# Float32 products of one transform stage replaced by three products of 12-bit parts

## The chip, the cores and the metric

One core of one Trainium2 chip. The metric is the device time of one execution in microseconds (us), lower is better. Runs of one kernel are compared by their medians.

## The reference

Two independent layers on inputs of 2048 positions and 512 features; their outputs are concatenated.

```python
def _A_ref(x, dft_seq_re, dft_seq_im, dft_hid_re, dft_hid_im):
    a = jnp.einsum("bsd,ed->bse", x, dft_hid_re)
    b = jnp.einsum("bsd,ed->bse", x, dft_hid_im)
    return jnp.einsum("ts,bse->bte", dft_seq_re, a) - jnp.einsum("ts,bse->bte", dft_seq_im, b)

def _B_ref(u, log_A_real, A_imag, C_real, C_imag, log_dt, D_skip):
    L = u.shape[1]
    dt = jnp.exp(log_dt)
    A = -jnp.exp(log_A_real) + 1j * A_imag
    C = (C_real + 1j * C_imag) * dt[:, None]
    P = jnp.exp((A * dt[:, None])[:, :, None] * pos[None, None, :])
    K = 2.0 * jnp.einsum("dn,dnl->dl", C, P).real
    Kf = jnp.fft.rfft(K, 2 * L)
    Uf = jnp.fft.rfft(u_t, 2 * L)
    y = jnp.fft.irfft(Uf * Kf[None, :, :], 2 * L)[:, :, :L]
    return y.transpose(0, 2, 1) + u * D_skip[None, None, :]
```

A multiplies x by two given matrices from both sides. B builds a long convolution kernel K from 128 exponentials per feature and convolves u with it. u has 2048 x 512 float32 values.

## The kernel before

Both layers run at once on the core. The Python program simulates a schedule while it emits instructions: each piece of work is a generator that yields either an event or a semaphore to wait for, or a pair of an engine and an assumed duration. `Plan.run` takes, again and again, the piece that can start first, and among those of equal start the one of lower urgency number (line 125). The order of the instructions on every engine is thus fixed by these assumed durations when the program is written; at run time each engine's queue runs in that order and waits on hardware semaphores. A generator's urgency is the second argument of `spawn`.

**Layer A, class `Fnet`.** Eight groups of sequence products ("s", sixteen blocks of 128 each) and four groups of hidden products ("p", eight blocks each). Every float32 operand is split into a high part rounded to the type `float32r` (ACT, line 184) and the rest, also `float32r` (DVE, line 188). Three products, high by high, high by low and low by high, are added in PSUM (line 304): one block of the moving operand is used for four 128-column slices of the stationary one, so twelve matmuls of 128x128 by 128x512. x is split once and stays in SBUF; the matrices stream through. `loads` (line 242) holds a buffer named "uk" of B's pool for x in flight, four blocks deep, and gives it back (`b.uks`, line 239) when all sixteen blocks of x are split. Splits have urgency 0, or 3 when three blocks or more are split ahead; the matmuls have urgency 5, and fill PE whenever nothing else is ready.

**Layer B, class `Ssm`.** In order of dependence:

- `tables` (urgency 2) with `seed_args` (1), `seeds`, `tables1` and `tables2`: for each of sixteen chunks of 32 features, powers of the exponentials, built on DVE by products and sums (lines 543 and 552) from seeds on ACT (lines 586 to 604) and their signed copies (line 618).
- `taps`: the values of K, sixteen times 128 small matmuls (line 739); `stage1_k`: the first transform stage of K (line 769) and its store.
- `spectrum_u` (urgency 2) and `stage1_u` (urgency 1), the part that is changed: the first transform stage of u. There are eight groups k. A group loads an eighth of u (512 KB, line 808) into one of two halves of a tile, takes two PSUM buffers of two banks each, does four float32 matmuls (line 814), evacuates them on ACT (four activations of 128x512, line 824), and stores them (line 830). The matrix `f1u` is stacked twice over the partitions, and the two halves of the rows work on different data: `tile_position=(64 * r, 0)`, each into its own bank.
- `products`: for four quarters h of the features and four parts q: loads (line 867), the second stage on PE (line 894), the complex product on DVE (lines 909 to 922), the first inverse stage (line 929) and a store (line 950).
- `inverses`: load, last stage (line 975), evacuation and store of the output (line 984).

B has two PSUM buffers in all, shared by `taps`, `stage1_k`, `stage1_u`, `products` and `inverses`; `banks` (line 415) hands them out in the order of asking. Of the buffers "uk", "z", "zl" and "xt" in B's pool there is one each until the tables are done, and two each in a second pool after that. `products` needs "uk" too.

All loads and most stores go through SP's queue, in the order of the plan.

Of the kernel before, what the change touches and what calls it, by code (L numbers as in the profile page):

```python
# [8 lines left out]
F32 = mybir.dt.float32  # L9
F32R = mybir.dt.float32r  # L10
I32 = mybir.dt.int32
AF = mybir.ActivationFunctionType
OP = mybir.AluOpType
# [3 lines left out]
SEQ, DM, NS = 2048, 512, 128  # L17
# [128 lines left out]
def act(cols):  # L146
    return 0.09 + cols * 0.00085


def dve(cols, rate=1.0):  # L150
    return (62 + cols / rate) / 960


def load(kb):
    return max(0.55, kb / 330)
# [210 lines left out]
class Ssm:  # L366
# [38 lines left out]
    def constants(self, which, ev):  # L405
        yield "dma", sum(load(4 * math.prod(a.shape) / 1024) for _, _, a in self.cst[which])
        for n, t, a in self.cst[which]:
            self.nc.sync.dma_start(t, a)
            setattr(self, n, t)
        if ev is self.const_ev:  # L410
            yield "dve", 0.3
            self.nc.vector.tensor_scalar(self.dskip, self.dskip, 0.5, None, op0=OP.mult)
        self.plan.set(ev)
# [376 lines left out]
    def spectrum_u(self):  # L790

        self.uleft = 16
        yield self.const_ev
        b = self.sets[0]
        yield b.zls
        self.xu_sb, self.xus = b.pool.tile([128, 2, 2, DM], F32, name="zl", bufs=b.n), Sem(2)
        for k in range(8):
            name = "uk"[k % 2]
            yield b.xts[name]
            if not k:  # L800
                self.u_sb = b.pool.tile([128, 2, 2, DM], F32, name="xt", bufs=b.n)
            self.plan.spawn(self.stage1_u(k, name), 1)

    def stage1_u(self, k, name):
        nc, b = self.nc, self.sets[0]
        u = self.u_sb[:, k % 2]
        yield "dma", load(512)
        nc.sync.dma_start(u, self.uG[:, 2 * k:2 * k + 2])
        got = yield from self.banks(2)
        yield "pe", 1.82  # L810
        for m in range(2):
            for r in range(2):
                rows = slice(64 * r, 64 * r + 64)
                nc.tensor.matmul(got[m][1][:, r], self.f1u[rows], u[rows, m], start=True, stop=True,  # L814
                                 tile_position=(64 * r, 0))
        self.plan.put(b.xts[name])
        for m in range(2):
            n = 2 * k + m
            sem = b.zbs if n % 3 == 2 else self.xus
            yield sem  # L820
            x = b.pool.tile([128, 2, DM], F32, name="z", bufs=b.n) if n % 3 == 2 else self.xu_sb[:, n % 3]
            for r in range(2):
                yield "act", act(512)
                nc.scalar.activation(x[:, r], got[m][1][:, r], AF.Copy)
            self.give(got[m][0])
            self.plan.spawn(self.store_u(x, 2 * k + m, sem), 1)

    def store_u(self, x, m, sem):
        yield "dma", load(512)
        self.nc.sync.dma_start(self.xu.rearrange("s c l d -> (s c) l d")[:, 2 * m:2 * m + 2], x)  # L830
        self.plan.put(sem)
        self.uleft -= 1
        if not self.uleft:
            self.plan.put(self.sets[0].zls)
            self.plan.set(self.xu_ev)

    def quarters(self):
# [225 lines left out]
```

## Time and profile before

| | us |
|---|---|
| median of 3 runs | 588.68 |
| lowest, highest | 588.62, 590.52 |
| the profiled execution | 590.22 |
| its span in the profile | 588.4 |

The profile shows one execution. PE is TensorE, PEld its weight loads, DVE VectorE, ACT ScalarE, POOL GpSimd, SP the engine whose queue issues the transfers. `L814` is line 814 of the kernel. A row of a group names the line, engine, operation, output and inputs by the program's names (tiles of one pool that share a name show as one: u in SBUF is `xt`, and the PSUM buffers are `f`), the shape, the count, the busy time and the mean of one in ns, and then the idle time of the engine just ahead of them with what ended it. A float32 matmul shows as two records. In the order of time a row has start, duration, engine, line, operation, and in brackets the idle time ahead of it. In the chain of waits a row has start, duration and what ran.

The granted clock of PE is 1.00 throughout.

### The profile page before, as it was taken

How to read it: one execution, taken by the hardware profiler on the slowest of the kernel's cores; microseconds unless marked ns; L12 is line 12 of the kernel's file. 1: busy time of each engine (PE TensorE's matmuls, PEld its weight loads, DVE VectorE, ACT ScalarE, POOL GpSimd, SP SyncE). 2: the span in 40 equal slices, each digit the busy share in tenths (PEclk: the TensorE clock that was granted, in tenths of full speed). 3: DMA queues.
4: the chain of work that ended last, by engine and by line, in shares of the span. 5: the costliest groups of instructions: out<-in, count | busy, mean ns of one | idle time of the engine just before them, and what ended most of it. 6: DMA issues, size and time to landing. Idle time of an engine off the chain costs nothing.

```text
span 588.4 us, 14902 instructions
## 1 busy us (share of the span) xinstructions
PE 580.2 (99%) x5958; PEld 439.7 (75%) x5958; DVE 496.5 (84%) x883; ACT 380.8 (65%) x745; POOL 4.7 (1%) x12
## 2 busy tenths in 40 slices
PE   8999999999999999999999999999999999999997
PEld 6767668778778777877687778777877776876785
DVE  7986989999999999999999999999999954245420
ACT  4789884946676677758674876577764635264622
POOL 0000000000000000000000000000000000000000
PEclk9999999999999999999999999999999999999999
DMA  8999996363493369446768684559798744998674
GB/s 262 329 367 338 337 342 199 101 188 81 122 280 106 89 170 264 137 135 165 246 183 259 168 246 128 136 158 284 225 282 234 230 131 148 283 354 263 190 251 144
DMA packets 141238, 125.84 MB, mean 214 GB/s; under 512 B 46192, under 2 KB 106352, under 8 KB 140912
## 3 DMA queue, kind: packets, MB, share of 16 engines
q1 hardware_dynamic: 140880, 124.48, 69.4%
q8 instruction: 47, 0.77, 0.5%
q10 hardware_dynamic: 288, 0.39, 0.2%
q14 instruction: 23, 0.19, 0.1%
HBM read 82.12 MB, written 42.73 MB: 212 GB/s over the span
## 4 chain that ended last, share of the span: by engine, by line
PE 69%; DVE 21%; issue 4%; DMA 3%; ACT 2%; SPq 1%; DVEq 0%; ACTq 0%
PE acc L304 52%; DVE prod L543 7%; DVE lo L188 4%; DVE t L552 4%; PE f L894 4%; PE f L739 3%; PE f L814 3%; PE f L975 3%; PE f L929 2%; PE f L769 2%; DMA xt<-xk 1%; DVE t L572 1%; DMA raw<-in_sT 1%; DVE t L566 1%; DVE cs L613 1%
## 5 line engine op out<-in xcount | busy, mean ns | idle before, releaser
L304 PE MATMUL acc<-hi,x_hi 128*128 128x512 f32 x640 | 257.2, 402 | 0.5 <-ACT x_hi L184 0.4
L304 PE MATMUL acc<-lo,x_hi 128*128 128x512 f32 x640 | 250.1, 391 | 1.5 <-issue 1.3
L304 PE MATMUL acc<-hi,x_lo 128*128 128x512 f32 x640 | 249.5, 390 | 0.1
L543 DVE TENSOR_TENSOR prod<-t,cs 128x1024 f32<-128x1024 f32 (+4 forms) x192 | 163.3, 869 | 3.6 <-ACT t L681 1.5
L188 DVE TENSOR_TENSOR lo<-raw,hi 128x512 fp32r<-128x512 f32 x160 | 109.1, 686 | 56.8 <-ACT hi L184 54.6
L304 PEld LDWEIGHTS acc<-hi,x_hi 128*128 128x128 f32 x640 | 120.1, 188 | 49.2 <-issue 21.2
L184 ACT ACTIVATE hi<-raw 128x512 fp32r<-128x512 f32 x160 | 100.1, 628 | 85.8 <-PE acc L304 64.7
L304 PEld LDWEIGHTS acc<-hi,x_lo 128*128 128x128 f32 x640 | 120.2, 188 | 28.0 <-issue 1.5
L304 PEld LDWEIGHTS acc<-lo,x_hi 128*128 128x128 f32 x640 | 120.2, 188 | 23.8 <-DVE lo L188 0.9
L552 DVE TENSOR_TENSOR t<-prod 128x512 f32<-128x512 f32 (+4 forms) x192 | 94.3, 510 | 1.1
L559 ACT ACTIVATE square<-t 128x256 f32<-128x256 f32 (+1 forms) x64 | 36.6, 572 | 24.6 <-DVE t L552 22.5
L327 ACT ACTIVATE y<-acc 128x512 f32<-128x512 f32 x47 | 27.9, 598 | 12.8 <-PE acc L304 9.5
L906 ACT ACTIVATE uk<-f 128x1024 f32<-128x1024 f32 x32 | 32.1, 1017 | 4.8 <-PE f L894 4.8
L739 PEld LDWEIGHTS f<-t,t 128*32 128x32 f32 x2048 | 29.4, 110 | 6.8 <-issue 4.1
L739 PE MATMUL f<-t,t 128*32 128x64 f32 x2048 | 32.2, 220 | 0.6 <-issue 0.6
L894 PE MATMUL f<-xt,w 64*32 64x256 f32 x1024 | 31.3, 379 | 0.0
L909 DVE TENSOR_TENSOR z<-uk 128x512 f32<-128x512 f32 x32 | 21.9, 685 | 8.3 <-ACT uk L906 4.7
L894 PEld LDWEIGHTS f<-xt,w 64*32 64x32 f32 x1024 | 18.4, 106 | 10.9 <-issue 4.6
L944 ACT ACTIVATE z<-f 128x512 f32<-128x512 f32 x32 | 17.6, 596 | 11.8 <-PE f L739 6.4
L572 DVE TENSOR_TENSOR t<-square 128x128 f32<-128x128 f32 (+1 forms) x64 | 24.6, 385 | 0.3 <-ACT square L559 0.3
L618 ACT ACTIVATE cs<-cs 128x352 f32<-128x352 f32 x32 | 15.9, 536 | 12.2 <-DVE cs L613 12.2
L911 DVE TENSOR_TENSOR uk<-uk 128x512 f32<-128x512 f32 x32 | 22.1, 690 | 0.8
(81 smaller groups left out, 409.7 us busy)
## 6 DMA issues: line engine op xcount, KB each, us to landing
raw<-in_sT SPq DMA_DIRECT2D x127, 256.0 KB, 3.3
p<-y SPq DMA_DIRECT2D x32, 256.0 KB, 4.1
xt<-xu SPq DMA_DIRECT2D x32, 256.0 KB, 4.4
xk<-xk_sb SPq DMA_DIRECT2D x32, 256.0 KB, 4.0
xt<-xk SPq DMA_DIRECT2D x32, 256.0 KB, 5.0
zs<-z SPq DMA_DIRECT2D x32, 256.0 KB, 3.4
zl<-zs SPq DMA_DIRECT2D x16, 512.0 KB, 5.9
raw<-p SPq DMA_DIRECT2D x32, 256.0 KB, 3.8
```

Of the source, the lines that this page charges most:

```text
L184: self.nc.scalar.activation(hi, src, AF.Copy)
L188: self.nc.vector.tensor_tensor(lo, src, hi.bitcast(F32), op=OP.subtract)
L304: nc.tensor.matmul(acc[d], l[:, cols], r, start=k == 0 and n == 0, stop=k == len(items) - 1 and n == 2)
L327: self.nc.scalar.activation(y, ps, AF.Copy, scale=-1.0 if g[2] == 1 else 1.0)
L543: self.nc.vector.tensor_tensor(p.rearrange("p k d c m -> p k (d c) m"), src.rearrange("p d c l -> p (d c) l")[:, None, :, rows].to_broadca ...
L552: self.nc.vector.tensor_tensor(dst[:, :, :, rows], p[:, 0], p[:, 1, :, ::-1], op=OP.add)
L559: self.nc.scalar.activation(sq, t[:, :, :, m // 2:m], AF.Square)
L572: self.nc.vector.tensor_tensor(t[:, :, 0, m:2 * m:2], box[0][:, :, 0], box[0][:, :, 1], op=OP.subtract)
L739: nc.tensor.matmul(ps[32 * j:32 * j + 32, i], t1[:, d, c], t2[:, d, c], start=c == 0, stop=c == 1, tile_position=(0, 32 * j))
L894: nc.tensor.matmul(both[:, :, c], self.w2[rows, 2 * q + r, xx, 32 * c:32 * c + 32], xt[rows, r, xx], start=True, stop=True, tile_position= ...
L906: a.activation(uk[:, r].rearrange("p g n c d -> p g (n c d)"), p, AF.Copy)
L911: v.tensor_tensor(t[:, r], t[:, r], u[:, r, :, ::-1], op=OP.mult)
```

## The change

u's blocks and the matrix `f1u` are each split into a high and a low part of type `float32r`: the matrix once, when it has been loaded, and u in each group, by one activation on ACT and one subtraction on DVE of 128x1024 each. Three products replace each float32 product, in the same banks, at the same tile positions. The parts of u share one tile from the pool of "uk", for which `spectrum_u` now waits, and which it gives back after the last store of the stage; a semaphore `u_free` lets one group at a time use the parts. The assumed duration of the matmuls in the plan goes from 1.82 to 1.42.

```diff
@@ constants
         if ev is self.const_ev:
+            self.f1u_hi = self.const.tile([128, 128], F32R, name="f1u_hi")
+            yield "act", act(128)
+            self.nc.scalar.activation(self.f1u_hi, self.f1u, AF.Copy)
+            yield "dve", dve(128)
+            self.f1u_lo = self.const.tile([128, 128], F32R, name="f1u_lo")
+            self.nc.vector.tensor_tensor(self.f1u_lo, self.f1u, self.f1u_hi.bitcast(F32), op=OP.subtract)
             yield "dve", 0.3
@@ spectrum_u
         yield b.zls
         self.xu_sb, self.xus = b.pool.tile([128, 2, 2, DM], F32, name="zl", bufs=b.n), Sem(2)
+        yield b.uks
+        self.u_hl, self.u_free = b.pool.tile([128, 2, 2, DM], F32R, name="uk", bufs=b.n), Sem(1)
@@ stage1_u
         nc.sync.dma_start(u, self.uG[:, 2 * k:2 * k + 2])
+        yield self.u_free
+        hi, lo = self.u_hl[:, 0], self.u_hl[:, 1]
+        yield "act", act(1024)
+        nc.scalar.activation(hi, u, AF.Copy)
+        yield "dve", dve(1024)
+        nc.vector.tensor_tensor(lo, u, hi.bitcast(F32), op=OP.subtract)
         got = yield from self.banks(2)
-        yield "pe", 1.82
+        yield "pe", 1.42
+        f_hi, f_lo = self.f1u_hi, self.f1u_lo
         for m in range(2):
-            for r in range(2):
-                rows = slice(64 * r, 64 * r + 64)
-                nc.tensor.matmul(got[m][1][:, r], self.f1u[rows], u[rows, m], start=True, stop=True,
-                                 tile_position=(64 * r, 0))
+            for n, (f, v) in enumerate(((f_hi, hi), (f_hi, lo), (f_lo, hi))):
+                for r in range(2):
+                    rows = slice(64 * r, 64 * r + 64)
+                    nc.tensor.matmul(got[m][1][:, r], f[rows], v[rows, m], start=n == 0, stop=n == 2,
+                                     tile_position=(64 * r, 0))
+        self.plan.put(self.u_free)
         self.plan.put(b.xts[name])
@@ store_u
         if not self.uleft:
             self.plan.put(self.sets[0].zls)
+            self.plan.put(self.sets[0].uks)
             self.plan.set(self.xu_ev)
```

## The prediction

> **What bounds the kernel now.** I read the page's first lines, then the busy time by stage, then the chain of waits at the end, then the order of time on DVE, ACT and SP around the two places that the chain pointed to.
>
> ```profile
> span 588.4 us, 14902 instructions
> PE 580.2 (99%) x5958; PEld 439.7 (75%) x5958; DVE 496.5 (84%) x883; ACT 380.8 (65%) x745; POOL 4.7 (1%) x12
> ```
>
> Busy time by stage (us of the stage, then busy us and instructions of each engine, granted clock, DMA share, GB/s):
>
> ```profile
> 20.00:40.00 20.00, 20.00 (x87) 14.25 (x86) 19.19 (x37) 16.47 (x35) 0.00 (x0) 1.00 0.95 332
> 40.00:50.00 10.00, 10.00 (x44) 6.87 (x45) 3.20 (x6) 9.94 (x20) 0.00 (x0) 1.00 0.97 350
> 50.00:80.00 30.00, 30.00 (x128) 19.79 (x128) 29.66 (x56) 27.69 (x62) 0.00 (x0) 1.00 0.98 339
> 80.00:110.00 30.00, 29.93 (x376) 23.04 (x373) 28.48 (x51) 19.46 (x43) 0.74 (x1) 1.00 0.58 201
> 110.00:480.00 370.00, 367.72 (x4253) 283.80 (x4255) 363.12 (x641) 249.44 (x497) 3.50 (x6) 1.00 0.65 186
> 480.00:589.00 109.00, 104.56 (x1025) 78.33 (x1013) 37.32 (x56) 47.28 (x76) 0.23 (x1) 1.00 0.74 228
> ```
>
> Two things are full. PE never idles until the end, because the Fnet products of line 304 run whenever the other half of the work (called B here) has no matmul ready. And DVE is full from 50 to 480 (363.12 of 370 in the long stage) with B's tables, then falls to a third. So there are two ends to watch: the sum of PE's work, and the chain that starts when DVE finishes the tables. The last table operation, on DVE in order of time, with the splits of Fnet behind it:
>
> ```profile
> 476.90 0.69 DVE L552 TENSOR_TENSOR t<-prod 128x512 f32<-128x512 f32 x1
> 478.03 0.69 DVE L188 TENSOR_TENSOR lo<-raw,hi 128x512 fp32r<-128x512 f32 x1 [0.45 <-ACT hi L184]
> 483.92 0.69 DVE L188 TENSOR_TENSOR lo<-raw,hi 128x512 fp32r<-128x512 f32 x1 [5.19 <-ACT hi L184]
> ```
>
> So the tables end at 477.6. What follows is a string of taps, stage one of k, a store and a load, four products with two PSUM banks between them, a store, a load and the inverse. Its last matmuls are line 975 in the chain of waits, and its last store is line 984 on SP's queue (two issues, the later one 3.87 us on, less its own issue), landing as in the list of transfers:
>
> ```profile
> 559.01 13.83 PE acc L304 x60
> 572.84 1.90 PE f L975 x32
> 574.74 1.58 PE acc L304 x6
> 576.32 1.90 PE f L975 x32
> 578.22 6.36 PE acc L304 x27
> ```
>
> ```profile
> 575.90 3.87 SPq L984 DMA_DIRECT2D out_yb<-zl  x2
> ```
>
> ```profile
> out_yb<-zl SPq DMA_DIRECT2D x2, 512.0 KB, 3.4
> ```
>
> The last store of B is issued at about 579.4 and lands at about 582.8. Fnet's last 6.36 us of matmuls end at 584.6, and its stores close the span at 588.4. I allow 1.0 us between the last landing and the end of the span, so B alone would end the span at 583.8. B's chain has a slack of 588.4 - 583.8 = 4.6 us against PE's sum, and that is the number on which this change turns.
>
> **The matmuls.** The stage is eight groups of line 814, all shown alike; the first in the chain of waits, and the form of its instructions:
>
> ```profile
> 27.78 1.92 PE f L814 x8
> ```
>
> ```profile
> L814 PEld LDWEIGHTS f<-xt,f1u x64: 182/186/187, 27.7 to 79.7; 64*128 64x128 f32 x64
> L814 PE MATMUL f<-xt,f1u x64: 589/589/693, 27.7 to 80.1; 64*128 64x512 f32 x64
> ```
>
> A group has four float32 products in eight records; 8 records of 589 ns inside 1.92 us means that the two row halves run side by side. So a group is four pairs of records, 0.48 us a pair. Line 304 shows what a product of 12-bit parts costs in a stream: 13.83 / 60 = 0.231 us for 512 columns. A new group is six pairs of such products: 6 x 0.231 = 1.39, and 0.10 for the first weights, as the first record of a group now takes 693 instead of 589. That is 1.49, 0.43 less than 1.92, and over eight groups **3.4 us off PE's sum**. The best is 3.6: a float32 record pair holds two passes of 512 columns, so (1.92 - 0.10) / 8 = 0.227 a pass, six passes and 0.10 make 1.47. The worst is a loss, if such products don't pair up by rows, which no row shows for them: 12 x 0.231 + 0.10 = 2.87, eight times 0.95 more, 7.6 us. I take the gain, since line 814 pairs today with the same tile positions.
>
> By the Trainium skill, "FP8 and Floating Point Precision", section "TensorE Precision Notes", a true float32 product is four passes through the array, of the high and low parts crosswise. The change keeps three of the four; by that rule a group would be three quarters of 1.92, 1.44, and the gain 3.8 us instead of 3.4. The row agrees so far that a pair of records takes twice a product of line 304.
>
> **The splits.** Each group adds one activation of 128x1024 on ACT and one subtraction of 128x1024 on DVE. The rows nearest to them: ACT's line 906 has the size, line 184 half of it with the same output type; on DVE a product of that size and what starts after it.
>
> ```profile
> L184 ACT ACTIVATE hi<-raw 128x512 fp32r<-128x512 f32 x160 | 100.1, 628 | 85.8 <-PE acc L304 64.7 <-issue 11.2 <-DMA raw<-in_sT 6.7
> L906 ACT ACTIVATE uk<-f 128x1024 f32<-128x1024 f32 x32 | 32.1, 1017 | 4.8 <-PE f L894 4.8
> ```
>
> ```profile
> 55.91 1.22 DVE L543 TENSOR_TENSOR prod<-t,cs 128x1024 f32<-128x1024 f32 x1
> 57.05 0.42 DVE L566 SCALAR_TENSOR_TENSOR t<-t 128x256 f32<-128x256 f32 x1
> ```
>
> ACT: 8 x 1.02 = 8.2 us (at most 8 x 1.26, two of line 184). DVE: the next starts 1.14 after, so 8 x 1.14 = 9.1, and the matrix's own split of 128 columns, under 0.3 on each engine: **9.4 us more on DVE**. This lies beside PE's work, but DVE is full until 477.6 and u's splits go ahead of the tables (urgency 1 against 2), so what finds no idle time there moves the tables back.
>
> **Where the stage goes.** The new wait for `b.uks` holds u back until the last of Fnet's sixteen x blocks is split, as these share the buffer. Today the first load of u is issued at 20.57, and x is done at 39.8:
>
> ```profile
> 20.57 0.33 SPq L808 DMA_DIRECT2D xt<-in_uG  x1
> ```
>
> ```profile
> 39.12 0.69 DVE L188 TENSOR_TENSOR x_lo<-uk,x_hi 128x512 fp32r<-128x512 f32 x1 [0.28 <-ACT x_hi L184]
> ```
>
> ```profile
> DMA to landing us min/median/max: 5.0/5.8/6.8
> ```
>
> With u's traffic gone from that stage (DMA share 0.95) I expect x some 3 to 4 us sooner, at about 36. The load takes 5.0 (last row, line 808), so u's first split starts near 41 and its first matmuls near 43.5, 15 us later than now. Queued behind the waiting process is only u's own work; on ACT, which runs in order, the seeds and copies of the tables stand behind each split of u, and a late load of u would hold them up too. The wait itself costs nothing: PE fills 27 to 43 with line 304, and nobody needs u before the first products.
>
> ```profile
> L830 SPq DMA_DIRECT2D xu<-zl x11: 326/405/579, 32.6 to 89.9; - x11
> ```
>
> ```profile
> L894 PE MATMUL f<-xt,w x1024: 376/376/400, 169.2 to 551.2; 64*32 64x256 f32 x171
> ```
>
> The last store goes from 89.9 to 105 or 110; the products start at 169.2. That cover would have to shrink by 60 us to count.
>
> **What DVE can absorb.** From 40 to 50 DVE is busy for 3.20 of 10, because the first tables wait for two copies of `cs` (line 618, urgency 2) behind u's evacuations and the seeds on ACT:
>
> ```profile
> 41.80 0.69 DVE L188 TENSOR_TENSOR lo<-raw,hi 128x512 fp32r<-128x512 f32 x1
> 46.90 0.69 DVE L188 TENSOR_TENSOR lo<-raw,hi 128x512 fp32r<-128x512 f32 x1 [4.42 <-ACT hi L184]
> 48.88 0.69 DVE L188 TENSOR_TENSOR lo<-raw,hi 128x512 fp32r<-128x512 f32 x1 [1.29 <-ACT hi L184]
> 50.07 0.89 DVE L613 TENSOR_TENSOR cs<-seed 128x704 f32<-128x704 f32 x1 [0.49 <-ACT seed L604]
> ```
>
> ```profile
> 41.95 0.53 ACT L618 ACTIVATE cs<-cs 128x352 f32<-128x352 f32 x1
> 49.91 0.54 ACT L618 ACTIVATE cs<-cs 128x352 f32<-128x352 f32 x1
> ```
>
> At u's pace (seven or eight us a group) up to three splits fall in or at the edge of that hole: 3 x 1.14 = 3.4. The rest, 9.4 - 3.4 = 6.0, delays the tables. While they are late Fnet goes on, and its splits take DVE time as well:
>
> ```profile
> 110.00:480.00 370.00, 75.95 (x112) 1.00 0.65 186
> ```
>
> Line 188 is 75.95 of 370 us there, or 112 slots of 0.61 (its start-to-start, an estimate from 0.686 less the 0.08 by which 1.22 exceeds 1.14), 0.185 of the time; so 6.0 / (1 - 0.185) = **7.4 us** later. B's end: 583.8 + 7.4 = 591.2, behind PE's sum of 588.4 - 3.4 = 585.0; PE then idles while B finishes, and what it saved is lost. Span 591.2.
>
> The profiled execution took 590.22 us around its span of 588.4; the median of the runs is 588.68, 0.3 above that span. I add the 0.3: **591.5 us**, 0.5% slower.
>
> **Rivals.** *Absorbed, faster.* The hole at 42 to 50 is one queueing accident on ACT: with u's evacuations moved away from 27 to 42, the second line 618 can run at 41 instead of 49.91, and the tables start 7 to 8 us sooner. Then 9.4 less about 8 is 1.4, or 1.7 with Fnet's splits; B ends at 585.5, PE's sum at 585.0. Time 585.3 to 585.8. It decides from a delay under 2.8 us (for 0.3%). For it: 6.8 us idle in one stage. Against it: ACT is at 9.94 of 10 there, and u's first split and evacuation arrive at that very time.
>
> *Half absorbed.* A delay of 5 us: 588.8 and 0.3, 589.1, no change.
>
> *Nothing absorbed.* ACT takes 9.94 + 27.69 + 19.46 = 57.1 of the 70 us from 40 to 110 now. With 8.2 of splits, and with the evacuations that lie between 20 and 40 today (line 824 by stage):
>
> ```profile
> 20.00:40.00 20.00, 3.22 (x6) 1.00 0.95 332
> ```
>
> it has 68.5 of 70. The tables' inputs then wait on ACT again, the hole stays, and 9.4 / 0.815 = 11.5 gives 595.3 and 0.3: 595.6.
>
> *No pairs.* The 7.6 us of loss above on PE's sum: 596.0 and 0.3, 596.3.
>
> *Loads not hidden.* If a weight load waited for the matmul of its own rows, a pair would cost 0.231 + 0.186, a group 2.50, 0.58 more than now: 4.6 us over eight groups, 593.0 and 0.3, 593.3. By the Trainium skill, "TensorE: Matmul & The Clock Gate", Part 3, "The mechanism", loads overlap matmuls in flight only where the row group differs, which would make this so. Line 304 uses all rows for both and still takes 0.231, so the trace disagrees, and I give it little.
>
> **Chances.** Forecast 0.43, absorbed 0.27, half absorbed 0.15, nothing absorbed 0.09, no pairs 0.04, loads not hidden 0.02. A measurement of this kernel can tell about 0.3% from no change, so 586.9 and 590.4 are the bounds: faster 0.27, same 0.15 and 0.02 from the forecast's lower edge, slower the rest, 0.56. The range takes in the absorbed case with the best matmul price and most of the slow ones: 585.0 to 596.2. The forecast's own range is 590 to 594.
>
> **What would show it.** Line 814 records near 390 ns, twelve a group, a group near 1.5 us; the first one near 43; DVE's splits of u at 1.14 each; the last line 552 near 485; PE idle, some 5 us or more, among the last line 894 to 975 groups, and the span closed by B's last store and not by Fnet's. If the last line 552 is at 480 or before, the hole absorbed the splits and I am wrong on the side of faster; if line 304 still runs behind the last line 975, PE's sum and not the tables sets the end.

## The result, and the profile after

| | before | after |
|---|---|---|
| median of 6 runs each, us | 589.75 | 596.87 |
| lowest, highest | 588.62, 592.38 | 594.47, 600.31 |
| the profiled execution | 590.22 | 600.31 |
| its span | 588.4 | 598.4 |

The ratio of the changed kernel to the one before is 1.0117 [1.0076, 1.0158]: slower, by 6.9 us at that ratio (the two medians differ by 7.1). The forecast was 591.5 and the range ended at 596.2. The direction was right; the loss is more than twice as large as forecast. The mechanism of the forecast is in the traces at about its size, and a second one that the prediction passed over lies on top of it.

The page of the changed kernel: the span, the busy time of the engines, and the queue that brings PE's instructions (transfers, MB, share).

```profile
span 598.4 us, 14990 instructions
...
PE 583.1 (97%) x5990; PEld 445.7 (74%) x5990; DVE 504.5 (84%) x892; ACT 389.0 (65%) x754; POOL 5.1 (1%) x12
...
q8 instruction: 47, 0.77, 0.5%
```

PE is busy for 580.2 us before and 583.1 after, and idle for 8.2 us before and 15.3 after. Of the 10.0 us of span 7.1 were lost by waiting. The other 2.9 are not more work, as the changed products take less (below); PE's mean granted clock fell from 1.000 to 0.991. The busy time by stage of the changed kernel, with the columns of the prediction:

```profile
20.00:40.00 20.00, 20.00 (x89) 16.24 (x88) 19.43 (x42) 14.89 (x37) 0.00 (x0) 1.00 0.84 303
40.00:50.00 10.00, 10.00 (x45) 7.99 (x44) 10.00 (x23) 9.15 (x17) 0.00 (x0) 1.00 0.89 296
...
110.00:480.00 370.00, 363.50 (x4140) 278.38 (x4140) 354.63 (x627) 254.58 (x505) 3.87 (x6) 0.99 0.64 191
```

The hole on DVE at 40 to 50 is gone (10.00 busy for 3.20). The long stage, which was full on both engines, is not any more: PE has 363.50 for 367.72 and DVE 354.63 for 363.12.

**The stage that was changed.** The instructions of its lines by form in the changed kernel (a row: min, median and max duration in ns, then first and last start): the two splits, the matmuls and the stores.

```profile
L820 ACT ACTIVATE uk<-xt x8: 1042/1048/1082, 53.6 to 128.2; 128x1024 fp32r<-128x1024 f32 x8
L822 DVE TENSOR_TENSOR uk<-xt,uk x8: 1218/1222/1226, 55.1 to 130.4; 128x1024 fp32r<-128x1024 f32 x8
L830 PE MATMUL f<-uk,f1u_hi x64: 385/391/499, 57.5 to 133.6; 64*128 64x512 f32 x64
L830 PE MATMUL f<-uk,f1u_lo x32: 385/388/395, 58.1 to 133.9; 64*128 64x512 f32 x32
L847 SPq DMA_DIRECT2D xu<-zl x11: 320/327/418, 62.0 to 137.3; - x11
```

The first of the groups in the changed kernel's chain of waits:

```profile
57.56 1.59 PE f L830 x12
```

One after the other, twelve products would take 2.77 us by line 304's 0.231; inside 1.59 us they run side by side by rows and hide their loads. A group takes 1.59, not the 1.49 of the sum, against 1.92 before: 8 x 0.33 = 2.6 us off PE. The stage lies 30 us later than before (27.7 to 57.5), not 15, and its last store is issued at 137.3, still 36 us ahead of the first products (line 912, at 173.0).

**The tables.** DVE in order of time in the changed kernel: the first table operation, the last split of x, and the last table operation.

```profile
41.36 0.68 DVE L549 TENSOR_TENSOR prod<-t,cs 128x128 f32<-128x128 f32 x2
...
44.55 0.69 DVE L188 TENSOR_TENSOR x_lo<-uk,x_hi 128x512 fp32r<-128x512 f32 x1
...
492.11 0.68 DVE L558 TENSOR_TENSOR t<-prod 128x512 f32<-128x512 f32 x1
```

The tables now start at 41.4 (50.9 before). x is done at 45.2, later than before (39.8) and not sooner. They end at 492.8, 15.2 us later than before (477.6) and not 7.4. Where these 15.2 us come from is to be read from the busy time up to the tables' end, cut at 300. Before:

```profile
0.00:300.00 300.00, 296.23 (x2750) 223.68 (x2751) 283.80 (x525) 213.17 (x436) 2.56 (x8) 1.00 0.69 214
300.00:477.60 177.60, 177.03 (x2092) 136.08 (x2091) 174.71 (x303) 119.92 (x233) 1.88 (x3) 1.00 0.71 206
```

After:

```profile
0.00:300.00 300.00, 296.29 (x2732) 229.00 (x2733) 288.96 (x525) 219.19 (x440) 2.99 (x8) 1.00 0.66 210
300.00:492.80 192.80, 187.02 (x2175) 142.92 (x2174) 179.76 (x314) 124.59 (x241) 1.87 (x3) 0.98 0.67 200
```

DVE's work to that point is 458.5 before and 468.7 after: 10.2 more. Its idle time to 300 falls from 16.2 to 11.0, which is the hole: 5.2 less. From 300 on its idle time rises from 2.9 to 13.0, 10.2 more. 10.2 - 5.2 + 10.2 = 15.2. The first two terms are those of the forecast (9.4 and 3.4). The third is not in it. In the same rows PE is idle from 300 on for 0.6 us before and for 5.8 after.

**The third term.** PE in order of time in the changed kernel, around the taps of three chunks (a row joins instructions of one form; in brackets the idle time ahead):

```profile
314.85 1.97 PE L745 MATMUL f<-t,t 128*32 128x64 f32 x123
318.54 0.31 PE L745 MATMUL f<-t,t 128*32 128x64 f32 x5 [1.71 <-issue]
...
350.29 1.99 PE L745 MATMUL f<-t,t 128*32 128x64 f32 x127
354.17 0.24 PE L745 MATMUL f<-t,t 128*32 128x64 f32 x1 [1.90 <-issue]
...
408.71 1.86 PE L745 MATMUL f<-t,t 128*32 128x64 f32 x115
412.62 0.42 PE L745 MATMUL f<-t,t 128*32 128x64 f32 x13 [2.04 <-issue]
```

In each of the three groups PE stops in the middle of 128 matmuls that depend on nothing new, "issue" being time in which it waits for nothing that the profile shows. Together 5.65 us. DVE in order of time, right behind the second and the third:

```profile
356.26 0.83 DVE L549 TENSOR_TENSOR prod<-t,cs 128x128 f32<-128x128 f32 x2 [4.22 <-ACT t L687]
...
414.89 0.40 DVE L549 TENSOR_TENSOR prod<-t,cs 128x128 f32<-128x128 f32 x1 [2.24 <-ACT t L687]
```

The next chunk's tables stand until ACT's line 687 has filled a buffer `t` that is not free before the taps have read it. So a stop of PE inside the taps is a stop of DVE. From 300 to the tables' end, DVE's lists of waits (us in total, times, longest) have before and after:

```profile
DVE prod L543 <- ACT t L681: 0.5, 1, 0.5
```

```profile
DVE prod L549 <- ACT t L687: 8.1, 3, 4.2
```

The third of PE's gaps lasts from 410.57 to 412.62. The list of transfers of the changed kernel in the window 410 to 411, where a transfer counts by its start, has:

```profile
q8 instruction: 1, 0.02, 6.4%
```

A block of instructions for PE arrives around the start of the gap. 6.4% of 16 engines for 1 us is 1.02 us; the trace has it from 410.16 to 411.18, and PE goes on at 412.62, 2.45 us after the transfer's start. In the other two gaps these are 2.24 and 2.23 us. 0.77 MB in 47 transfers is 16 KB each, and 5990 products and 5990 loads over 47 transfers are 255 instructions each. The taps of one chunk are 128 loads and 128 products in some 1.95 us, so they can use up a whole block in less time than passes from the start of a transfer until PE goes on. By the Trainium skill, "Runtime: NRT & Kernel Launch", section "Instruction fetch mechanics", instructions come in 16 KiB blocks of 256, which these rows show, and the fetch is hidden because the issue of instructions is slower than the fetch; in these three groups the rows disagree. Rows of this kind were in the trace before too, in its list of PE's waits from 110 to 480, and I passed over them:

```profile
PE acc L304 <- issue: 1.3, 1, 1.3
PE f L739 <- issue: 0.6, 1, 0.6
```

**The end.** The changed kernel's chain of waits at its end, and its last store on SP in order of time:

```profile
586.29 1.90 PE f L993 x32
588.19 1.58 PE acc L304 x6
589.77 1.90 PE f L993 x32
591.67 0.91 PE acc L304 x3
```

```profile
593.77 0.38 SPq L1002 DMA_DIRECT2D out_yb<-zl  x1
```

B's last product ends at 591.67, 98.9 us after the tables; before it was 578.22 - 477.6 = 100.6. The tail of B has nearly its old length. Its last store lands at about 597.5 and closes the span, as forecast. But PE doesn't idle there: three products of Fnet are left over behind B.

### The profile page after: what moved, and what is told of

It reads as the page before. It is cut to its first block, busy times and chain, and to the rows that moved or that the text cites. A ratio compares the mean times of both kernels' runs of the same rounds, so it can differ in the third digit from the quotient of the medians.

```text
span 598.4 us, 14990 instructions
## 1 busy us (share of the span) xinstructions
PE 583.1 (97%) x5990; PEld 445.7 (74%) x5990; DVE 504.5 (84%) x892; ACT 389.0 (65%) x754; POOL 5.1 (1%) x12
## 4 chain that ended last, share of the span: by engine, by line
PE 83%; DVE 6%; ACT 4%; issue 3%; DMA 2%; SPq 0%; ACTq 0%; DVEq 0%
PE acc L304 65%; PE f L912 5%; PE f L745 5%; PE f L947 3%; PE f L993 3%; DVE prod L549 2%; PE f L775 2%; PE f L830 2%; DVE t L558 1%; DVE lo L188 1%; DMA xu<-zl 1%; ACT y L327 1%; ACT hi L184 1%; DMA uk<-in_x 1%; DVE t L578 0%
## 5 line engine op out<-in xcount | busy, mean ns | idle before, releaser
L549 DVE TENSOR_TENSOR prod<-t,cs 128x1024 f32<-128x1024 f32 (+3 forms) x192 | 164.1, 871 | 10.0 <-ACT t L687 8.3
L304 PEld LDWEIGHTS acc<-lo,x_hi 128*128 128x128 f32 x640 | 121.5, 190 | 24.7 <-DVE lo L188 1.5
L327 ACT ACTIVATE y<-acc 128x512 f32<-128x512 f32 x47 | 27.9, 595 | 14.2 <-PE acc L304 13.4
L962 ACT ACTIVATE z<-f 128x512 f32<-128x512 f32 x32 | 17.8, 595 | 17.8 <-PE f L745 10.7
L784 ACT ACTIVATE xk_sb<-f 128x512 f32<-128x512 f32 x32 | 17.3, 599 | 8.2 <-PE f L775 8.2
```

The source lines that it names most:

```text
L304: nc.tensor.matmul(acc[d], l[:, cols], r, start=k == 0 and n == 0, stop=k == len(items) - 1 and n == 2)
L327: self.nc.scalar.activation(y, ps, AF.Copy, scale=-1.0 if g[2] == 1 else 1.0)
L549: self.nc.vector.tensor_tensor(p.rearrange("p k d c m -> p k (d c) m"), src.rearrange("p d c l -> p (d c) l")[:, None, :, rows].to_broadca ...
```

## The experiments

Two theories stand against each other in most of the runs. One, the blocks of instructions (F in the expectations), says that the splits and the move of the stage cost what the forecast has, and that the rest of the loss is PE's stops in the taps, set by where these 256 instructions fall in the stream of blocks. The other, the work of the splits (D), says that the splits on DVE cost the whole of it, and that the stops are chance or a consequence.

**The changed kernel once more.** No edit.

> The changed kernel once more, for a second profile. Theory F (fetch): PE's three gaps of 1.7 to 2.0 us inside the 10th, 11th and 13th tap group (line 745) are waits for the next 16 KB block of its instructions; they come at the same three groups again, their sizes differ a little, and the end of the tables moves with their sum: 594 to 600 us, tables end 485 to 493. Theory D (DVE): the delay is all work of the splits on DVE, the tables end at 492 to 493 whatever PE's gaps are, and the time stays within 1 us of the median 596.9.

596.26 us, 1.0105 [1.0089, 1.0121]; the tables end at 488.5. PE stops in the same three groups of taps, 1.45, 2.16 and 0.92 us, 4.53 in sum. The places are the program's, the sizes vary: 1.1 us less of stops goes with 4.3 us less of tables. But 2.0 of the 4.3 were there when the tables began, at 39.4 for 41.4: in the first profile Fnet's products start 0.43 us apart until 10.7, and 0.23 after that, in the second until 7.0 only.

**PE's stream moved.** Three warm-up products at the start of Fnet become two and N small ones, so that everything behind them stands 4N - 4 loads and products later in PE's stream and does nothing else. N is 50 and 55 in the changed kernel (196 and 216 later), 35 in the kernel before (136).

```diff
-        for n in range(3):
-            self.nc.tensor.matmul(ps[:, :256], z[:, :128], z[:, 256:], start=n == 0, stop=n == 2)
+        for n in range(2):
+            self.nc.tensor.matmul(ps[:, :256], z[:, :128], z[:, 256:], start=n == 0, stop=n == 1)
+        for n in range(N):
+            j = 32 * (n % 4)
+            self.nc.tensor.matmul(ps[j:j + 32, 256:320], z[:, :32], z[:, 256:320], start=True, stop=True,
+                                  tile_position=(0, j))
```

> The changed kernel with 196 more PE instructions ahead of the first product (50 small products in the warm-up in place of its third one), the order of all else unchanged, so that the tap groups fall elsewhere in the 256-instruction blocks. F: no gap over 1 us in any tap group, tables end near 483, 590 to 592.5 us. D: nothing changes, tables end 492 to 493, 595 to 598 us.

591.91 us, 1.0032 [1.0022, 1.0042], 4 to 5 us less than the changed kernel, with the same work and the same order. One stop is left in the taps, 0.59 us; the tables end at 483.5. The first of the three groups, which stood from 316.83 to 318.54, now has its 128 matmuls in one row; PE in order of time:

```profile
314.68 1.99 PE L749 MATMUL f<-t,t 128*32 128x64 f32 x128
316.61 0.50 PE L308 MATMUL acc<-hi,x_hi 128*128 128x512 f32 x1
```

> The kernel of before with 136 more PE instructions in the warm-up in the same way. F: three to five tap groups (the 2nd, 5th, 13th and 16th by their place in the blocks, perhaps the 8th) now stand for 1 to 2 us, the two gaps of before at 286 and 371 go away, the tables end 3 to 9 us later and the time is 591 to 598 us. D: same as before, 588.5 to 590.5 us.

589.29 us, 0.9982 [0.9968, 0.9996]. This missed: the stops of the kernel before, at 286 and 371, went, and only one other came, 0.77 us at 395. So a place that looked bad from the changed kernel's trace doesn't always give a stop. That the edit itself costs nothing is seen here too.

**More places.** N = 17 and 40 in the kernel before, 55 and 38 in the changed one.

> The kernel of before with 64 more PE instructions in the warm-up (17 small products for its third one), so that 1 of the 16 tap groups starts at place 145 to 200 of a 256-instruction block, where 18 of 36 groups stood in the ten profiles so far. Theory F (fetch): at most one gap over 0.5 us in a tap group, 587.5 to 589 us. Theory D (order and DVE alone decide): as before, 589 to 590.5.

589.79 us, 0.9988 [0.9973, 1.0003], one stop of 1.18 us; no difference from the kernel before. The stop is as theory F has it, the time lies in D's range.

> The kernel of before with 156 more PE instructions (40 small products): 7 of the 16 tap groups start at place 145 to 200. F: three to five gaps over 0.5 us in tap groups, 3 to 5 us in sum, tables end 2 to 5 us later than in before, 591 to 595 us. D: as before, 589 to 590.5.

590.61 us, 1.0003 [0.9985, 1.0021], one stop of 1.69 us. Missed again: more stops were expected.

> The changed kernel with 148 more PE instructions (38 small products): 6 of its 16 tap groups start at place 145 to 200, 4 of them before 320 us. F: three or more gaps over 0.5 us, tables end 485 to 492, 593 to 599 us. D: as the changed kernel, 595 to 598, without a tie to the gaps.

594.73 us, 1.0072 [1.0048, 1.0095]. Its profiled execution shows two stops, 1.17 and 0.39, and the tables end at 484.2: fewer than expected, and more time than the places that were meant to be good.

> The changed kernel with 216 more PE instructions (55 small products): none of its 16 tap groups starts at place 145 to 200. F: no gap over 0.5 us in a tap group, tables end at 482 to 484, 590.5 to 592 us. D: 595 to 598.

590.95 us, 1.0009 [0.9993, 1.0024]: no difference from the kernel before that can be measured. In its list of waits PE has no stop from 300 to 480. Its busy time up to the tables' end:

```profile
0.00:300.00 300.00, 296.56 (x2845) 230.64 (x2845) 289.88 (x528) 219.74 (x441) 2.99 (x8) 1.00 0.67 211
300.00:482.40 182.40, 182.24 (x2170) 139.97 (x2169) 178.19 (x311) 124.17 (x241) 1.92 (x3) 1.00 0.71 210
```

DVE's work is 468.1, 9.6 more than before; its idle time 14.3, 4.8 less; the tables end at 482.4, 4.8 later. The idle time to 300 falls by 6.1 (the hole), and from 300 on it grows by 1.3, where the changed kernel has 10.2. So the third term is nearly gone, and the tables' delay is about what the first two make. The end of its chain of waits and its last store on SP:

```profile
581.28 1.90 PE f L997 x32
583.17 0.91 PE acc L308 x3
```

```profile
585.28 0.38 SPq L1006 DMA_DIRECT2D out_yb<-zl  x1
```

B's last store is issued at 585.3, 5.9 later than before (579.4).

Five executions have the changed kernel's order, apart from the place of PE's stream:

| kernel | stops in taps, us | tables end | its own time |
|---|---|---|---|
| 216 later | 0 | 482.4 | 591.84 |
| 196 later | 0.59 | 483.5 | 591.44 |
| 148 later | 1.56 | 484.2 | 593.06 |
| as changed, second profile | 4.53 | 488.5 | 596.41 |
| as changed, first profile | 5.65 | 492.8 | 600.31 |

The more PE stops in the taps, the later the tables end, by (492.8 - 482.4) / 5.65 = 1.8 us a us. The rows show why it is more than one. Up to the tables' end PE is idle for 9.5 us in the changed kernel and for 3.6 in the one 216 later, 5.9 more; and it is busy for 483.3 and 478.8, 4.5 more, without more work. Together that is the 10.4. Most of the 4.5 comes after two of the three stops, where PE ran at half clock for a while. The changed kernel's windows behind the stops at 352 and 411:

```profile
350.00:360.00 10.00, 8.10 (x204) 5.84 (x194) 4.28 (x10) 3.34 (x10) 0.00 (x0) 0.83 0.73 200
410.00:420.00 10.00, 7.96 (x131) 5.65 (x120) 6.32 (x13) 3.35 (x9) 0.00 (x0) 0.83 0.39 110
```

0.83 of 10 us is 3.4 us at half rate, 1.7 lost each time. By the Trainium skill, "TensorE: Matmul & The Clock Gate", Part 1, the clock is decided by windows of 3.41 us and halves after an idle one; the length agrees, but stops of 1.9 and 2.0 us were enough here.

I then counted PE's loads and products up to the start of each group of taps, modulo 256, over all sixteen profiles of this study (256 groups):

| place of the group's start | groups | with a stop over 0.4 us | stops in sum, us |
|---|---|---|---|
| 0 to 144 | 151 | 2 | 2.5 |
| 145 to 199 | 49 | 21 | 25.1 |
| 200 to 255 | 56 | 1 | 2.0 |

The three groups of the changed kernel start at 171, 157 and 171; in the kernel that is 216 later they start at 131, 117 and 131. The three outside the window do not bear on it: two are waits for DVE (1.68 and 1.61, in the kernel with POOL), and one (0.81) is a stop of the kind below. The window was read off the first ten profiles (18 of 36 groups there had a stop) and then stood in the expectations of the six later ones, where 3 of 13 had one. So the place is not enough by itself: 28 of the 49 groups had no stop worth counting. In three of those (starts at 155, 157 and 171, in the two profiles of the question) a block's transfer had started 1.5 to 2.5 us ahead of the group; in another, at 157 in the kernel before, it had not.

A finer count over the packed traces tells more. If PE's semaphore instructions are counted with its loads and products, all 22 stops without a wait in or just behind a group of taps (0.39 to 2.16 us) begin at the same place, after record 193 of a block of 256, and so does the one of 0.81. The n-th of these places goes with the n-th transfer. At none of the 739 places in the sixteen profiles did PE go on sooner than 2.16 us after the start of its transfer, or sooner than 1.20 after its end. So in these stops PE waits for its next block. How long it stops goes with when the transfer starts: in the six stops of the changed kernel's two profiles, 0.2 us after the group's start goes with a stop of 0.92, and 1.1 to 1.9 us with stops of 1.45 to 2.16.

**The move alone.** The kernel before, with the new wait and the return of the buffer, without splits.

```diff
         self.xu_sb, self.xus = b.pool.tile([128, 2, 2, DM], F32, name="zl", bufs=b.n), Sem(2)
+        yield b.uks
...
             self.plan.put(self.sets[0].zls)
+            self.plan.put(self.sets[0].uks)
```

> The kernel of before with only the wait for the buffer of x (and its return at the end of the stage), so that u's stage starts after x, with its float32 products and no splits. If the late stage is what costs: tables end after 483. If the splits' work costs and the late stage helps (DVE's hole at 42 to 50 goes away): tables end near 472 to 473 plus the gaps of PE's instruction fetch, PE's sum sets the end, 588 to 591 us with the gaps.

592.36 us, 1.004 [1.0023, 1.0057]. The tables end at 474.0, 3.6 sooner, and DVE is busy for 9.96 of the 10 us from 40 to 50: it is the move that closes the hole. The time is longer all the same, by PE's sum: 0.70 and 1.57 us of stops in the taps and 0.75 outside them, and after the last group of B (575.17) there are 9.76 us of Fnet's products still to do, where the kernel before had 6.36. The tables ended about as the second expectation had it, the time 1.4 us above its range.

**The splits without the cheaper matmuls.** The changed kernel with the four float32 products in place of the twelve, and their 1.82 in the plan.

```diff
-        yield "pe", 1.42
-        f_hi, f_lo = self.f1u_hi, self.f1u_lo
+        yield "pe", 1.82
         for m in range(2):
-            for n, (f, v) in enumerate(((f_hi, hi), (f_hi, lo), (f_lo, hi))):
-                for r in range(2):
-                    rows = slice(64 * r, 64 * r + 64)
-                    nc.tensor.matmul(got[m][1][:, r], f[rows], v[rows, m], start=n == 0, stop=n == 2,
-                                     tile_position=(64 * r, 0))
+            for r in range(2):
+                rows = slice(64 * r, 64 * r + 64)
+                nc.tensor.matmul(got[m][1][:, r], self.f1u[rows], u[rows, m], start=True, stop=True,
+                                 tile_position=(64 * r, 0))
```

> The changed kernel with the four float32 products of before on u itself (1.82 us in the plan); the parts of u and of the matrix are still made, and not used. If what PE saves is lost in the tail, as forecast: within 1.5 us of the changed kernel for equal gaps, tables end 483 plus the gaps of its own (new places in the blocks). If PE's sum sets the end: 2.6 us slower than the changed kernel.

603.13 us, 1.0223 [1.0196, 1.025], 6 to 7 us above the changed kernel: a miss. The tables end at 495.0, and DVE's idle time to that point is 24.0, half of the stretch from 100 to 120 among it (9.45 busy of 20). The assumed 0.4 us more of a group makes a plan of another order, in which the tables wait at that place. This run therefore doesn't isolate the matmuls.

**Most of the splits taken out.** Only the first of the eight groups splits its u; the other seven multiply the first group's parts, so seven splits on each engine are left out and all matmuls stay.

```diff
-        yield "act", act(1024)
-        nc.scalar.activation(hi, u, AF.Copy)
-        yield "dve", dve(1024)
-        nc.vector.tensor_tensor(lo, u, hi.bitcast(F32), op=OP.subtract)
+        if not k:
+            yield "act", act(1024)
+            nc.scalar.activation(hi, u, AF.Copy)
+            yield "dve", dve(1024)
+            nc.vector.tensor_tensor(lo, u, hi.bitcast(F32), op=OP.subtract)
```

> The changed kernel with u split in the first group only; the other seven groups multiply the first group's parts (their own u is loaded and not used). So the late stage and the cheaper products stay, and seven of eight splits (8 us of DVE, 7.3 of ACT) go. If the splits' work on DVE is the cost: tables end near 474 to 476 plus gaps, PE's sum sets the end, 585.5 to 587.5 us and up to 2 us more with gaps. If the cost lies elsewhere: 591 to 597 us as the changed kernel.

591.72 us, 1.0013 [0.9997, 1.003]. DVE's work to the tables' end is 459.2, 9.5 less than in the changed kernel (468.7), of which seven splits of 1.22 are 8.5. The tables end at 481.7 and not near 475, since DVE idles 22.5 us, 7.8 of them from 100 to 120, and PE stops in or behind two groups of taps (0.76 and 1.38) and waits 0.98 for ACT's line 327 at 281. By its time the run falls on the side of a cost elsewhere. But the splits' work went as it should, and its gain was eaten by idle time that belongs to another order, so this run bounds nothing finer.

**The subtraction on POOL.**

```diff
-        yield "dve", dve(1024)
-        nc.vector.tensor_tensor(lo, u, hi.bitcast(F32), op=OP.subtract)
+        yield "pool", 2.4
+        nc.gpsimd.tensor_tensor(lo, u, hi.bitcast(F32), op=OP.subtract)
```

> The changed kernel with the subtraction of each group on POOL, which is idle, in place of DVE. If DVE's work is the cost and POOL does not slow DVE down: tables end near 474 to 476 plus gaps, 585.5 to 588.5 us, under both kernels. If POOL's subtraction holds DVE up while it runs (a shared port): as the changed kernel or worse, 591 to 597 us, and DVE's instructions beside it are longer than their usual 1.22 and 0.69.

601.73 us, 1.02 [1.0171, 1.0229]. The subtraction on POOL, and the products of the tables on DVE in the first 140 us (groups by line and form: busy time, mean ns), in this kernel:

```profile
L822 POOL TENSOR_TENSOR uk<-xt,uk x8: 2403/2564/6150, 52.7 to 136.8; 128x1024 fp32r<-128x1024 f32 x8
```

```profile
L549 DVE TENSOR_TENSOR prod<-t,cs 128x1024 f32<-128x1024 f32 x20 | 30.6, 1529 | 0.3
```

The same group in the changed kernel:

```profile
L549 DVE TENSOR_TENSOR prod<-t,cs 128x1024 f32<-128x1024 f32 x21 | 25.6, 1221 | 0.2
```

The mean of a product is 1.53 us for 1.22 in the stretch in which POOL works beside it; over 20 of them that is 6.2 us given back, of the 9.8 that eight splits take on DVE, and the splits of line 188 go from 0.69 to 0.79 as well. By the Trainium skill, "GPSIMD Engine Reference", section "1. Specifications", POOL shares its SBUF interface with DVE and contends with DVE instructions that have two SBUF inputs; these rows agree. The time is above both ranges: the tables end at 492.5, and PE, which waits for DVE and POOL here, idles 13.4 of the first 300 us.

**u behind the tables.** Urgency 3 in place of 1 for the stage, so that its splits fill what the tables leave.

```diff
-            self.plan.spawn(self.stage1_u(k, name), 1)
+            self.plan.spawn(self.stage1_u(k, name), 3)
```

> The changed kernel with u's groups at urgency 3 in place of 1, after the tables, so that their splits take DVE when it is otherwise idle. As DVE has some 11 us idle from 10 to 300 in the changed kernel but mostly in pieces under 1 us, the delay stays: 590 to 597 us, tables end 480 to 490. If the order on DVE were the cost and not the sum: tables end near 476, 586 to 588 us.

593.12 us, 1.0052 [1.0025, 1.0079]. The tables end at 468.6, 9 us sooner than before, with only 9.6 us idle on DVE. But u's last store is at 203.5, and the first products at 215.1, where they were at 169.2: the cover that the prediction called safe is used up here. B's last products wait for a load, in its chain of waits:

```profile
575.92 7.12 DMA zl<-zs
583.08 2.00 PE f L993 x16
```

They end 116 us after the tables, in place of some 100: 16 of B's 32 stores of `z` (line 950 of the kernel before) are still to come when the tables end, where it was 12. So the tables' end is not the only thing that sets B's end: u must be done in time.

**Between the two.** Urgency 2 with N = 3 (8 later), and urgency 1.5 with N = 58 (228 later).

> The changed kernel with u's groups at urgency 2, level with the tables, and 8 more PE instructions so that none of its tap groups starts at place 145 to 200 of a block. If the delay left without gaps (tables end 482.4, B's last store 5 us later than before) comes from u's splits going ahead of the tables, and can be given back by order: tables end 474 to 479, u's stage ends by 150, 586 to 588.5 us, under both kernels. If it is the sum of DVE's work, or u's lateness then holds up the products as at urgency 3: 589.5 to 593.

593.23 us, 1.0054 [1.0033, 1.0076]. The tables end at 478.9, but PE idles 7.2 us up to 300, 2.3 of it at 226, and PE's sum sets the end.

> The same with urgency 1.5, between the seeds (1) and the tables (2), and 228 more PE instructions, none of its tap groups at place 145 to 200. By order: the seeds come earlier on ACT, u's splits still ahead of the tables; tables end 479 to 482, 587.5 to 590 us. By the sum of the work: 589.5 to 592.

601.98 us, 1.0184 [1.0161, 1.0207]; two of its six executions took 826 and 2019 us, for which no trace here shows a reason, the others 600.2 to 602.3 with a median of 601.1. The tables end at 495.3 with 23.0 us idle on DVE, and B's last products wait 7.1 us for a load. This missed, and the order made by an urgency between the two is the worst of the three. No kernel of this study with a change to u's stage is faster than the one before.

## Why the prediction was right and wrong

- *Matmuls.* Pairs run side by side and the loads are hidden, so the two rivals on them fell. A group takes 1.59 for the 1.49 of the sum: 2.6 us off PE and not 3.4. By the rule of four passes, which the prediction cites from the Trainium skill ("FP8 and Floating Point Precision", section "TensorE Precision Notes"), it would be 1.44, and the rows are further from it.
- *Splits.* 1.05 on ACT and 1.22 on DVE, as costed; the work on DVE up to the tables' end grows by 9.6 to 10.2, the sum had 9.4.
- *The stage's place.* x was expected done at 36 and was at 45.2, so the stage came 30 us later and not 15. The move alone has x done at 44.0, so it is not the splits that hold x up; what does is open. The cover to the first products held.
- *The hole.* It gave back 5.2 to 6.1, the sum had 3.4, but in another way: the tables start at 41.4, as the rival "absorbed" had it, and fill it themselves. The move alone shows this (9.96 of 10). None of u's splits falls there; the first is at 55.1.
- *Sum of these.* 4.8 us of delay where no stop came, and B's last store 5.9 later, against 7.4. That kernel takes 590.95, 0.1% [-0.07, 0.24] more than before; the forecast was 591.5. The kernel before has 1.9 us of stops itself; against its variant with one stop of 0.77 (136 later, 0.9982) the loss is 0.3%.
- *The step that failed.* The prediction has "PE never idles until the end", and one cause for a delay, that DVE is full and "what finds no idle time there moves the tables back". So PE's own stops stand in its sum as nothing, though the rows of before have two of them, 1.9 us. The changed kernel has 5.65 us of these in three groups of taps, with 3.4 us at half clock behind each of two, and 10.2 us more of idle time on DVE. From 300 to the tables' end PE's idle time is 5.8 us, nearly all of it these stops: there the tables wait for PE, and PE never for the tables. Moving PE's stream by 216 instructions takes these stops away and 5.3 to 5.9 us of the 6.2 to 6.9 us that the changed kernel loses.
- *What would show it.* B's store does close the span. PE's 5 us of idle time among the last groups is not there, since PE lost as much before and has products left.
- *The near rival.* "Nothing absorbed" has 595.6, near the measured time, but for a reason that is not there: ACT did not hold the tables, and the hole closed. "No pairs" has 596.3, nearer still, and fell with the 1.59 of a group. That either is close to 596.9 is chance.

Open is why a block's transfer starts at different times behind the start of the same group, and in most groups early enough. Open is also what the 4.8 us of delay without stops are due to. On DVE they add up from the splits' work and the hole, but PE is as full there (0.2 us idle from 300 to 482.4), and its new order leaves 301 of Fnet's 1,920 products behind the tables' end, where 333 were: 32 more come ahead of it. No run changed DVE's work and kept that order. Also open is what makes DVE idle at 100 to 120 in the orders of two of the kernels.

## What to carry to other kernels

Where an engine runs some hundred short instructions in a burst, read its gaps that wait for nothing, and look for an instruction transfer that ends inside them: a change of a few dozen instructions anywhere ahead moves all later bursts against the blocks, and can cost or save as much as the change itself. To tell the two apart, run the changed kernel again with its stream moved by some harmless instructions, at several places, before its loss is put down to its work. In a schedule written out ahead, a small change of an assumed duration makes another order, so an experiment that changes one is no experiment on one part.

## What was not expected of the hardware

- PE can stop for 0.4 to 2.2 us at the end of a block of 256 instructions, when 256 loads and products run in some 1.95 us: it went on 2.16 us or more after the start of the next block's transfer at all 739 block ends of sixteen profiles.
- Stops of 1.9 and 2.0 us are followed by 3.4 us at half clock (0.83 in a window of 10 us). In all sixteen profiles before 570 us, the five stops of PE of 1.9 to 2.3 us have such a stretch behind them, and none of those up to 1.8 us has.
- A subtraction of 128x1024 on POOL takes a median of 2.56 us, and one of the eight 6.15.
